# Attention with a feed-forward behind it on one core: the first quad laid out anew, row-norm seeds, transposes and sums moved in the instruction order

**Chip, cores, metric.** One Trainium2 chip (trn2), one of its cores. The metric is the time of one execution in microseconds (us), as the median of several executions; lower is better. Names in profile lines: PE is TensorE (matrix products), PEld its weight loads, DVE is VectorE, ACT is ScalarE, POOL is GpSimd, SPq the queue of SyncE that issues loads. In names of tiles, qk is a pair's loaded q and k, qkn the same normalised, qkT transposed, s its scores, E their exponentials, o its outputs; rc holds the reciprocals of the sums, xT the divided outputs, u and uT the hidden values of the feed-forward and their transposition. The gain of a pair is the scaling of its q by the gains. A clock window is here a stretch of 3.4 us, or a few of them in a row, for which TensorE was granted half its clock. Lanes are slots that loads in flight take up; no trace names them. Every line number is that of the kernel whose profile the line is from; the changed kernel's numbers are about 5 above those of the kernel before.

## The reference, cut to what matters

```python
# q, k, v: (8 batches, 12 heads, 448, 64) fp32;  x: 3584 tokens x 768;  d_ff = 1024
q_n, k_n = rmsnorm(q, g_q), rmsnorm(k, g_k)          # x / sqrt(mean(x*x) + 1e-6) * g
attn = softmax(q_n @ k_n.T / sqrt(64))               # per head
x = (attn @ v) in (batch * seq, heads * 64)
h = x @ w_in
solu = h * softmax(h)
ln = (solu - mean) / sqrt(var + 1e-6) * g_ln
out = ln @ w_out                                     # fp32
```

## The kernel before

It works on head pairs n (48 of them) and on quads m of two pairs, a = 2m and b = 2m + 1. TensorE goes through a quad's scores, values and sums. The other three engines meanwhile prepare the next quad's pairs: squares (ACT), row sums (DVE), a swap of halves and a fold (POOL), the seed of an inverse root (ACT), its step and the normalising (POOL), a transposition (DVE) and the scaling by the gains (ACT), behind which the first scores of a pair wait. They also divide the last quad's outputs and convert pieces of the weights (`begin`, `step`, `end`). From quad 6 on the feed-forward of finished tokens is mixed in, as units of TensorE work with ACT and DVE work behind them.

These are the operations that the change moves:

```python
    def first(n):
        return nc.gpsimd if n else nc.vector

    def swap_sums(n):                                  # row sums of the other half: 4 POOL copies
        d = st[n]
        d["ss"] = small.tile([P, 2 * NB], FP32, tag="ss", name="ss")
        for g in range(4):
            o = g ^ 1
            first(n).tensor_copy(d["ss"][g * 32 : g * 32 + 32], d["part"][o * 32 : o * 32 + 32])

    def fold_sums(n):
        d = st[n]
        first(n).tensor_tensor(d["ss"], d["ss"], d["part"], OP.add)

    def rsqrt_seed(n):                                 # 3 small ACT instructions
        # ... cut
        nc.scalar.activation(d["y"], d["ss"], AF.Ln, scale=1.0 / D, bias=eps)
        nc.scalar.activation(d["x"], d["ss"], AF.Copy, scale=-0.5 / D, bias=-0.5e-6)
        nc.scalar.activation(d["y"], d["y"], AF.Exp, scale=-0.5)

    def inverse(m):                                    # DVE, then 4 POOL copies
        # ... cut
        nc.vector.transpose(r.rearrange("p b i -> p (b i)"), d["sm"])
        nc.vector.reciprocal(rc, r[:, :, 0].rearrange("p b -> p () b").to_broadcast([P, 2, NB]))
        for h in range(2):
            for i in range(2):
                a = 64 * h + 32 * i
                o = 64 * h + 32 * (1 - i)
                nc.gpsimd.tensor_copy(rc[o : o + 32, i], rc[a : a + 32, i])
```

The order of the quad loop, which is the order in which each engine's queue gets its instructions (`W_IN` = 12 and `W_OUT` = 22 are the pairs at which w_in and w_out are converted, so `a < W_OUT` means quads 0 to 10):

```python
            unit(lambda: scores(b, 2))                 # ends with the last exponential of b
            # ... adds cut
            if next1:
                if m:
                    rsqrt_seed(a + 2)
                    rsqrt_step(a + 2)
                    normalise(a + 2)
                rsqrt_seed(b + 2)
                rsqrt_step(b + 2)
            # ... cut: outputs, squares and sums of a + 4, qk_transpose(a + 2), normalise(b + 2),
            #          values(b), squares(b + 4), row_sums(b + 4), gain(a + 2)
            if next2:
                swap_sums(b + 4)
                fold_sums(b + 4)
            unit(lambda: sums(m))
            if a < W_IN and next1:
                qk_transpose(b + 2)
            inverse(m)
            if a >= W_IN and next1:
                qk_transpose(b + 2)
            later(1, lambda m=m: divide(m))            # after the next unit of TensorE work
```

The start, cut: `load_next()` loads one 512 KB piece of w_in.

```python
    load(0); setup(); load(1); load_next(); load_next()
    load(2); load(3); load_v(0); load_next()
    # ... 8 warming products on TensorE, then pairs 0 and 1 prepared, then the loop
```

## Time and profile before

| | before |
|---|---|
| median (the 3 runs that the prediction had) | 1006.16 us (1004.56 to 1006.8) |
| span of the profiled execution | 1004.8 us |
| mean granted clock of TensorE | 0.988 |
| first score product | 18.59 us |
| starts of quads 1, 6, 11 and 12 | 41.67, 123.14, 264.55 and 313.0 us |

A quad's start is its first score product in the timeline of PE. The distance of two starts is a quad's length, and the difference of two kernels' starts is how far one leads by then. The lines of the page, of the waits and of the timeline before stand in the prediction.

### The profile page before, as it was taken

How to read it: one execution, taken by the hardware profiler on the slowest of the kernel's cores; microseconds unless marked ns; L12 is line 12 of the kernel's file. 1: busy time of each engine (PE TensorE's matmuls, PEld its weight loads, DVE VectorE, ACT ScalarE, POOL GpSimd, SP SyncE). 2: the span in 40 equal slices, each digit the busy share in tenths (PEclk: the TensorE clock that was granted, in tenths of full speed). 3: DMA queues.
4: the chain of work that ended last, by engine and by line, in shares of the span. 5: the costliest groups of instructions: out<-in, count | busy, mean ns of one | idle time of the engine just before them, and what ended most of it. 6: DMA issues, size and time to landing. Idle time of an engine off the chain costs nothing.

```text
span 1004.8 us, 11376 instructions
## 1 busy us (share of the span) xinstructions
PE 958.6 (95%) x3907; PEld 431.9 (43%) x3907; DVE 515.3 (51%) x756; ACT 359.4 (36%) x622; POOL 294.0 (29%) x641
## 2 busy tenths in 40 slices
PE   6899898899899999999999999999999999999997
PEld 2232233333344444444444444454444444455554
DVE  3588866667545435454544453526254544466610
ACT  4778655546432323232322332323133233011110
POOL 3475742233423223232414131415141312100000
PEclk9899999999999999999999999999999999999999
DMA  7667653344303021212113030303030100455201
GB/s 153 135 161 137 143 123 82 74 94 87 55 23 65 24 47 34 54 33 54 36 35 71 16 71 16 70 3 71 16 71 16 34 17 19 166 157 159 84 34 49
DMA packets 235956, 70.14 MB, mean 70 GB/s; under 512 B 224968, under 2 KB 225232, under 8 KB 235888
## 3 DMA queue, kind: packets, MB, share of 16 engines
q1 hardware_dynamic: 227840, 57.77, 26.4%
q10 hardware_dynamic: 7888, 11.47, 3.0%
q8 instruction: 33, 0.54, 0.2%
q14 instruction: 35, 0.29, 0.1%
q0 software_dynamic: 160, 0.07, 0.1%
HBM read 58.27 MB, written 11.01 MB: 69 GB/s over the span
## 4 chain that ended last, share of the span: by engine, by line
PE 76%; DVE 8%; POOL 6%; ACT 4%; DMA 3%; issue 2%; SPq 1%; POOLq 0%; DVEq 0%; ACTq 0%
PE po L836 28%; PE h L778 26%; PE s L657 8%; PE o L711 7%; PE pu L825 2%; POOL qkn L626 2%; PE s L670 2%; POOL ss L600 2%; ACT E L647 1%; DVE r L758 1%; PE o L700 1%; DVE xT L760 1%; PE warm L957 1%; PE sm L735 1%; DMA qk<-in_k_dram 1%
## 5 line engine op out<-in xcount | busy, mean ns | idle before, releaser
L778 PE MATMUL h<-w_in,xT 128*128 128x512 f32 x672 | 303.8, 602 | 0.1
L836 PE MATMUL po<-w_out,uT 128*128 128x384 f32 x896 | 298.0, 489 | 1.4 <-ACT uT L826 0.7
L836 PEld LDWEIGHTS po<-w_out,uT 128*128 128x128 f32 x896 | 168.0, 190 | 131.5 <-issue 19.3
L647 ACT ACTIVATE E<-s 128x896 f32<-128x896 f32 x168 | 149.0, 914 | 163.9 <-PE s L657 158.9
L778 PEld LDWEIGHTS h<-w_in,xT 128*128 128x128 f32 x672 | 125.5, 192 | 161.1 <-issue 155.4
L657 PE MATMUL s<-qkT 64*128 64x448 f32 (+1 forms) x768 | 136.9, 574 | 18.8 <-ACT E L647 7.8
L837 ACT COPY y<-po 128x384 f32<-128x384 f32 x56 | 26.8, 478 | 266.9 <-PE po L836 266.9
L711 PE MATMUL o<-E,v 128*64 128x448 f32 x576 | 115.1, 549 | 1.7 <-ACT E L647 1.7
L809 POOL TENSOR_TENSOR he<-he,mhalf 128x1 f32<-128x1 f32 x28 | 18.7, 669 | 291.9 <-DVE he L808 291.7
L687 POOL TENSOR_TENSOR es<-E 128x896 f32<-128x896 f32 x26 | 54.0, 2076 | 147.3 <-ACT E L647 147.3
L690 DVE TENSOR_TENSOR es<-es,E 128x896 f32<-128x896 f32 (+1 forms) x52 | 56.6, 1089 | 64.0 <-ACT E L647 58.5
L657 PEld LDWEIGHTS s<-qkT 64*128 64x128 f32 (+1 forms) x768 | 42.6, 160 | 101.4 <-issue 45.0
L827 DVE COPY uT<-pu 128x512 f32<-128x512 f32 x28 | 19.2, 687 | 130.3 <-PE pu L825 79.2
L626 POOL TENSOR_TENSOR qkn<-qk,ny 128x896 f32<-128x896 f32 x47 | 80.6, 1714 | 10.8 <-DMA v<-in_v_dram 4.8
L788 DVE TENSOR_REDUCE hmax<-h 128x1 f32<-128x1024 f32 x28 | 34.2, 1221 | 77.0 <-PE h L778 77.0
L711 PEld LDWEIGHTS o<-E,v 128*64 128x64 f32 x576 | 39.5, 138 | 76.3 <-issue 67.8
L587 DVE TENSOR_REDUCE part<-sq 128x28 f32<-128x896 f32 x48 | 51.2, 1066 | 40.6 <-ACT sq L582 40.4
L618 POOL TENSOR_TENSOR nx<-nx,ny 128x28 f32<-128x28 f32 x47 | 19.8, 421 | 153.0 <-ACT ny L613 153.0
L636 DVE STREAM_TRANSPOSE qkT<-qkn 128x896 f32<-128x896 f32 x48 | 53.0, 1103 | 21.9 <-POOL qkn L626 21.2
L799 DVE TENSOR_TENSOR u<-h,u 128x1024 f32<-128x1024 f32 x28 | 34.2, 1221 | 50.7 <-ACT u L794 50.7
L582 ACT ACTIVATE sq<-qk 128x896 f32<-128x896 f32 x48 | 45.5, 949 | 36.6 <-DVE part L587 22.8
L758 DVE STREAM_TRANSPOSE r<-rc 128x448 f32<-128x448 f32 x48 | 30.9, 644 | 40.7 <-POOL rc L749 38.2
(90 smaller groups left out, 741.3 us busy)
## 6 DMA issues: line engine op xcount, KB each, us to landing
qk<-in_q_dram SPq DMA_DIRECT2D x192, 56.0 KB, 2.3
out_dram<-y ACTq DMA_DIRECT2D x27, 384.0 KB, 2.3
qk<-in_k_dram SPq DMA_DIRECT2D x184, 56.0 KB, 2.4
v<-in_v_dram SPq DMA_DIRECT2D x96, 96.0 KB, 2.6
raw<-in_moe_w_in_dram SPq DMA_DIRECT2D x12, 512.0 KB, 4.3
raw<-in_moe_w_out_dram SPq DMA_DIRECT2D x16, 384.0 KB, 3.1
again<-in_moe_w_in_dram SPq DMA_DIRECT2D x13, 448.0 KB, 3.9
again<-in_moe_w_out_dram SPq DMA_DIRECT2D x13, 448.0 KB, 4.1
```

Of the source, the lines that this page charges most:

```text
L582: nc.scalar.activation(d["sq"], d["qk"].rearrange("p s b d -> p (s b) d"), AF.Square)
L587: nc.vector.tensor_reduce(d["part"], d["sq"], AX, OP.add)
L626: first(n).tensor_tensor(d["qkn"], d["qk"].rearrange("p s b d -> p (s b) d"), d["y"].rearrange("p b -> p b ()").to_broadcast([P, 2 * NB, 32]),
L636: nc.vector.transpose(d["qkT"].rearrange("p s t -> p (s t)"), d["qkn"].rearrange("p b d -> p (b d)"))
L647: nc.scalar.activation(d["E", kc], s[:, :, 0:S], AF.Exp)
L657: nc.tensor.matmul(s[c : c + w, h, 0:S], d["qkT"][hh, 1, kc * P + c : kc * P + c + w], d["qkT"][hh, 0, :], start=True, stop=True,)
L687: engine.tensor_tensor(d["es"], d["E", 0], d["E", 1], OP.add)
L690: engine.tensor_tensor(d["es"][pp], d["es"][pp], x[pp], OP.add)
L711: nc.tensor.matmul(d["o"][h * D : (h + 1) * D, :], d["v"][:, h, kc], d["E", kc][:, h], start=False, stop=(kc == NJ - 1),)
L758: nc.vector.transpose(r, quads[m]["rc"][:, i].rearrange("p b -> p b ()").to_broadcast([P, NB, 32]))
L778: nc.tensor.matmul(d["h"][:, hs], xTs[m][:, c, i * P : (i + 1) * P], w_in[:, c, hs], start=(c == 0), stop=(c == KD - 1))
L836: nc.tensor.matmul(po, d["uT"][:, c], w_out[:, c, hs], start=(c == 0), stop=(c == KF - 1))
```

## The change

Its intent, in four parts. The first quad gets another order: gains loaded through ACT's queue, squares of pair 0 on DVE, no warming products, one piece of w_in fewer ahead of pairs 2 and 3 and one more behind the first values, pair 3 prepared in smaller steps. The seeds of both next pairs are issued ahead of the last exponential of b (from quad 1 on). The transposition of b's next pair goes ahead of the inverse in quads 6 to 10 too, as it did in quads 0 to 5. And swapping and folding of b's sums go behind the copies of the reciprocals.

The diff, whole:

```diff
@@ -438,13 +438,14 @@
         nc.gpsimd.memset(ones[0:D, 2], 0.0)
         make_identity(nc, ident)
 
+    def load_gains():
         for i, g in enumerate((g_q, g_k)):
-            nc.gpsimd.dma_start(gg[:, i], g.rearrange("(o d) -> o d", o=1).to_broadcast([P, D]))
-            nc.gpsimd.dma_start(
+            nc.scalar.dma_start(gg[:, i], g.rearrange("(o d) -> o d", o=1).to_broadcast([P, D]))
+            nc.scalar.dma_start(
                 grow[KF + i : KF + i + 1].rearrange("o (h d) -> o h d", h=2),
                 g.rearrange("(o d) -> o () d", o=1).to_broadcast([1, 2, D]),
             )
-        nc.gpsimd.dma_start(grow[0:KF, :], moe_g_ln.rearrange("(c p) -> c p", p=P))
+        nc.scalar.dma_start(grow[0:KF, :], moe_g_ln.rearrange("(c p) -> c p", p=P))
 
     def gain_columns():
         pg = ps_t.tile([P, KF + 2], FP32, tag="t", name="pg")
@@ -579,7 +580,11 @@
     def squares(n):
         d = st[n]
         d["sq"] = work.tile([P, 2 * NB, 32], FP32, tag="sq", name="sq", bufs=1)
-        nc.scalar.activation(d["sq"], d["qk"].rearrange("p s b d -> p (s b) d"), AF.Square)
+        qk = d["qk"].rearrange("p s b d -> p (s b) d")
+        if n:
+            nc.scalar.activation(d["sq"], qk, AF.Square)
+        else:
+            nc.vector.tensor_tensor(d["sq"], qk, qk, OP.mult)
 
     def row_sums(n):
         d = st[n]
@@ -935,28 +940,17 @@
 
     N = B * NP
 
-    def prepare(n):
-        squares(n)
-        row_sums(n)
-        swap_sums(n)
-        fold_sums(n)
-
     load(0)
     setup()
     load(1)
-    load_next()
+    load_gains()
     load_next()
     load(2)
     load(3)
     load_v(0)
     load_next()
+    load_next()
     with tc.manual_schedule():
-
-        warm = ps_h.tile([P, DFF], FP32, tag="h", name="warm")
-        for _ in range(8):
-            nc.tensor.matmul(
-                warm[:, 0:S], ident, st[0]["qk"][:, 1].rearrange("p b d -> p (b d)"), start=True, stop=True
-            )
         squares(0)
         row_sums(0)
         swap_sums(0)
@@ -964,21 +958,19 @@
         squares(1)
         row_sums(1)
         rsqrt_seed(0)
-        gain_columns()
-        begin(0)
         rsqrt_step(0)
-        nc.vector.tensor_reduce(gmax, gg[:, 0], AX, OP.max, apply_absolute_value=True)
-        normalise(0)
         swap_sums(1)
         fold_sums(1)
+        gain_columns()
+        normalise(0)
+        nc.vector.tensor_reduce(gmax, gg[:, 0], AX, OP.max, apply_absolute_value=True)
         gain_limit()
         rsqrt_seed(1)
         rsqrt_step(1)
         normalise(1)
         qk_transpose(0)
         gain(0)
-        step(0)
-        end(0)
+        begin(0)
         at = 0
         for m in range(NQ):
             a, b = 2 * m, 2 * m + 1
@@ -1005,6 +997,8 @@
                 step(a)
             else:
                 qk_transpose(1)
+                step(0)
+                end(0)
             unit(lambda: scores(a, 1))
             gain(b)
             if next2:
@@ -1018,10 +1012,10 @@
             if m:
                 end(a)
             else:
-                prepare(2)
-                rsqrt_seed(2)
-                rsqrt_step(2)
-                normalise(2)
+                squares(2)
+                row_sums(2)
+                swap_sums(2)
+                fold_sums(2)
             add(a, 2, DVE)
             ff(1)
             unit(lambda: scores(b, 0))
@@ -1031,23 +1025,26 @@
                 if a >= W_IN:
                     begin(b)
             else:
-                prepare(3)
+                squares(3)
+                row_sums(3)
             add(b, 1, POOL)
             add(a, 3, DVE)
             ff(2)
+            if m and next1:
+                rsqrt_seed(a + 2)
+                rsqrt_seed(b + 2)
             unit(lambda: scores(b, 2))
             add(b, 1, DVE)
             add(b, 3, DVE)
             add(b, 2, DVE)
+            if m == 0:
+                rsqrt_seed(2)
+                begin(1)
             if next1:
+                rsqrt_step(a + 2)
+                normalise(a + 2)
                 if m:
-                    rsqrt_seed(a + 2)
-                    rsqrt_step(a + 2)
-                    normalise(a + 2)
-                rsqrt_seed(b + 2)
-                rsqrt_step(b + 2)
-            if m == 0:
-                begin(1)
+                    rsqrt_step(b + 2)
             step(b)
             unit(outputs)
             if next2:
@@ -1056,6 +1053,11 @@
             end(b)
             if next1:
                 qk_transpose(a + 2)
+                if m == 0:
+                    swap_sums(3)
+                    fold_sums(3)
+                    rsqrt_seed(3)
+                    rsqrt_step(3)
                 if a < W_IN:
                     begin(a + 2)
                 normalise(b + 2)
@@ -1074,15 +1076,15 @@
                     begin(a + 2)
                 if b + 2 < W_IN:
                     begin(b + 2)
+            unit(lambda: sums(m))
+            if a < W_OUT and next1:
+                qk_transpose(b + 2)
+            inverse(m)
+            if a >= W_OUT and next1:
+                qk_transpose(b + 2)
             if next2:
                 swap_sums(b + 4)
                 fold_sums(b + 4)
-            unit(lambda: sums(m))
-            if a < W_IN and next1:
-                qk_transpose(b + 2)
-            inverse(m)
-            if a >= W_IN and next1:
-                qk_transpose(b + 2)
             later(1, lambda m=m: divide(m))
             if next1:
                 load_v(m + 1)
```

## The prediction

> **What bounds the kernel now.** I read the page's busy shares first, then who TensorE waited for in three stretches, then the timeline around the longest of those waits.
>
> ```profile
> span 1004.8 us, 11376 instructions
> PE 958.6 (95%) x3907; PEld 431.9 (43%) x3907; DVE 515.3 (51%) x756; ACT 359.4 (36%) x622; POOL 294.0 (29%) x641
> PE   6899898899899999999999999999999999999997
> ```
>
> TensorE (PE) bounds the kernel: it is busy for 958.6 of 1004.8 us, and from slice 12 on it has almost no idle time. What a reordering can win is the remaining 46 us, plus the 8.7 us of warming products that count as busy and do no work, plus whatever runs at half clock. Nearly all of it lies before 300 us, as the waits of PE show (us in total, times, longest) for 0 to 100 us, 100 to 300 and 300 to the end:
>
> ```profile
> PE s L657 <- ACT qkT L640: 5.5, 4, 2.6
> PE s L657 <- ACT E L647: 5.1, 5, 3.7
> ...
> PE s L670 <- ACT qkT L640: 9.4, 4, 2.9
> PE pu L825 <- DVE xT L760: 2.4, 2, 1.6
> ...
> PE s L657 <- DVE uT L827: 3.2, 3, 1.4
> ```
>
> The parts of the change answer to these waits one by one. A quad m is two head pairs, a = 2m and b = 2m+1. By its first score products, quad 0 runs from 18.59 to 41.67 us, quads 1 to 5 take 16.3 us each, quads 6 to 10 about 30 each with the feed-forward between, and from quad 11 (264 us) PE is full.
>
> **What the Trainium skill says.** "TensorE: Matmul & The Clock Gate", Part 1: the array is at half clock until a free-running window of about 3.4 us was busy, and goes back after an idle one. The trace agrees: the granted clock averages 0.84 in 20 to 30 us and 0.70 in 30 to 40, although eight products warmed the array up to 15.8 us; the first scores at 18.59 take 0.75 us a product, twice the later 0.37. It went cold in the 2.6 us gap behind the warming. The same page, "Architectural detail", calls the queues of ScalarE, VectorE and GpSimd strict FIFO; every argument below rests on that, and the trace shows it (the gain of b stands behind an exponential of the feed-forward, below). "SBUF — State Buffer", "Who interferes with whom": a VectorE instruction with two SBUF inputs, or in a 2-port mode, and a GpSimd instruction that reads SBUF exclude each other. The trace agrees: GpSimd's small multiply takes 0.24 us alone and 0.57 to 1.27 beside VectorE's sums of E.
>
> **Part 1, the first quad.** Here the chain is GpSimd and ScalarE order:
>
> ```profile
> 15.77 0.22 PE L451 MATMUL pg<-ident,grow 10*128 10x10 f32 x1
> 16.03 0.17 ACT L452 COPY gcol<-pg 128x10 f32<-128x10 f32 x1 [4.76 <-PE pg L451]
> 17.89 0.65 ACT L640 ACTIVATE qkT<-qkT,gcol 128x448 f32<-128x448 f32 x1
> 18.59 4.33 PE L657 MATMUL s<-qkT 64*128 64x448 f32 x16 [2.60 <-ACT qkT L640]
> ```
>
> The transposition of the gains waits for the warming products; behind its copy stand the weight conversion (1.4 us) and the seeds of b (0.55). The new order takes all three away from ahead of the gain, but puts five gain loads in ScalarE's queue ahead of the squares of pair 1. The last of these reuses the lane of k's last slice (issued 7.0, about 2.6 to land), so I put the squares at 10.2 instead of 9.73, row sums to 12.3, step 13.1, normalising 14.2, GpSimd's sums of pair 1 and the gain product 14.7, maximum 14.9, VectorE's transposition (1.1) 16.05, gain (0.65) 16.75: first scores at 16.8, 1.8 us earlier. Then the seeds of pair 2 no longer stand between the exponentials (PE waited 3.7 us there). With cold products of 1.5 us a score tile the last exponential of b ends near 28.6 instead of 32.8. But pair 3's sums still come on GpSimd behind the normalising of pair 2 (near 32.3) and ScalarE waits for them: seeds of 3 near 34.0, one conversion 1.4, squares of pair 5 0.95, gain 0.7, quad 1 at about 37.5. Loads give nearly the same bound: pair 5 landed about 35.4 before (last issue 33.1, 2.3 to land), same bytes ahead of it now, then squares and gain make 37.1. I take 38.0 for 41.67: **-3.7 us**. The missing warm-up costs nothing, since the scores were cold already.
>
> **Part 2, quads 1 to 5.** Between two quads:
>
> ```profile
> 45.42 0.89 POOL L749 COPY rc<-rc 32x14 f32<-32x14 f32 x4
> 46.09 0.65 DVE L758 STREAM_TRANSPOSE r<-rc 128x448 f32<-128x448 f32 x1 [1.31 <-POOL rc L749]
> ...
> 49.95 0.31 ACT L611 ACTIVATE ny<-ss,eps 128x28 f32<-128x28 f32 x1
> ...
> 57.13 0.67 ACT L640 ACTIVATE qkT<-qkT,gcol 128x448 f32<-128x448 f32 x1 [1.50 <-DVE qkT L636]
> ...
> 57.85 1.77 PE L657 MATMUL s<-qkT 64*128 64x448 f32 x8 [0.96 <-ACT qkT L640]
> ```
>
> The seeds move ahead of the last exponential (0.92 us), so they start at 49.1, not 49.95. That alone gives little: GpSimd's first step then meets VectorE's sum of E (49.79 to 50.87), and it ended at 50.97 already. The quieter edit matters more: swapping and folding b's sums now come behind the copies of the reciprocals, which were waiting for them. The reciprocal was done at 44.78, so the copies start at 44.85 instead of 45.42, and the whole VectorE chain of dividing, converting and summing moves 0.57 us up, the GpSimd step with it. PE's wait of 0.96 falls to about 0.4. Five starts (quads 2 to 6) at 0.57: **-2.85 us**.
>
> **Part 3, quads 6 to 10.** The wait of 9.4 us:
>
> ```profile
> 149.23 0.89 POOL L749 COPY rc<-rc 32x14 f32<-32x14 f32 x4
> 149.91 0.65 DVE L758 STREAM_TRANSPOSE r<-rc 128x448 f32<-128x448 f32 x1 [2.21 <-POOL rc L749]
> 152.54 1.21 DVE L788 TENSOR_REDUCE hmax<-h 128x1 f32<-128x1024 f32 x1
> 153.79 1.11 ACT L794 ACTIVATE u<-h,hmax 128x1024 f32<-128x1024 f32 x1 [2.10 <-DVE hmax L788]
> 154.90 0.66 ACT L640 ACTIVATE qkT<-qkT,gcol 128x448 f32<-128x448 f32 x1
> 155.60 1.76 PE L670 MATMUL s<-qkT 64*64 64x448 f32 x4 [2.90 <-ACT qkT L640]
> ```
>
> The gain is not late for want of the transposition, done at 147.7, but queued behind the feed-forward's exponential, and that behind maximum, dividing and reciprocal copies. Counted from T, the end of b's normalising (146.56), copies started at T+2.67 behind two sets of sums. Now: transposition 1.1, inverse 1.0 behind it, copies at T+2.2. So the new transposition order alone would cost a microsecond, and the copies ahead of the sums win it back and 0.49 more. T moves up too: seeds 0.8 earlier, of which about 0.45 arrives, because b's normalising waits for VectorE to transpose a (ended 144.73). Together 0.94 for each of four waits: -3.8. The wait of transposes on dividing at quad 11 has the same cause: -0.95. These idle times also sent the clock to one half for 3.4 us in quads 7, 8 and 9 (the mean is 0.94 in each; the last products take 1.76 us instead of 0.97, and the next group 6.16 and 7.10 instead of 5.42), about 1.5 us each; I count on two of the three: -3.0. One wait grows: in quad 10 values already wait 1.7 us for the last exponential, which comes 0.9 later, but dividing ends that stretch, so it is hidden. Sum **-7.75 us**.
>
> **Part 4, from quad 11.** The copies come 1.24 us earlier (0.92 and 0.24 with their gaps), the seeds about a microsecond. This should remove most of the waits on VectorE's copy of uT (3.2 us): **-2.2 us**. All else is PE at work.
>
> **Sum.** 3.7 + 2.85 + 7.75 + 2.2 = 16.5; 1006.16 - 16.5 = 989.7, say **990 us**, a gain of 1.6%.
>
> **Rivals.** (1) The first quad gains little. The gain loads in ScalarE's queue wait for lanes, squares of pair 1 slip, and loads or seeds of pair 3 hold quad 1. For it: ScalarE waited 2.7 us for GpSimd there, and DMA is 0.78 to 0.80 busy to 30 us. Then part 1 gives 0 to 1 and the time is 993. (2) The transposition ahead of the inverse stretches the dividing chain more than the copies save, because VectorE stands waiting for GpSimd's normalising. For it: the gap is only half a microsecond. Then part 3 gives 1 or 2 and the time is about 996. (3) All PE waits go, with their cold windows: 5.5 at the start, 4.75, 9.4 + 4.5 + 2.4, 3.2 make 30 us, 976 us. Against it: only some of each chain is shortened. (4) The last exponential, a microsecond later, stalls values in every quad. Against it: outside quad 10 it is needed only after 4 us of other products.
>
> **Range and chances.** The four terms err mostly alone, the clock windows by chance: 80% within **983.5 to 997.5**. Faster by over 2% means below 986.0, some 4 us under my figure: **0.22**. Within 2%: **0.77**. Slower: **0.01**; nothing is added to TensorE, VectorE gains one 1.1 us square and loses nothing.
>
> **What would show it.** First scores near 16.8 us and quad 1 near 38; quads 1 to 5 at 15.7 us each; copies of reciprocals directly behind the reciprocal; the 9.4 us wait near 5.6; clock below 1.0 in at most one or two windows between 150 and 250; PE busy about 950 us, 8.7 less by the warming. I am wrong if quad 1 starts after 40, if the 9.4 stays or vanishes, or if values wait for the last exponential in many quads.

## The result, and the profile after

The changed kernel takes **990.49 us** (median of 4, 990.15 to 991.6) beside 1006.21 (1004.56 to 1006.8, 4 runs) for the one before: ratio 0.9848, 95% interval 0.9831 to 0.9865. That is 1.5% faster, inside two per cent. The profiled execution spans 988.7 us, 16.1 less than before.

The head of the page of the changed kernel (busy us, share of the span, instructions; then PE's busy tenths in 40 slices):

```profile
span 988.7 us, 11291 instructions
PE 944.8 (96%) x3891; PEld 426.6 (43%) x3891; DVE 510.8 (52%) x757; ACT 355.3 (36%) x621; POOL 297.3 (30%) x636
PE   3699999998999999999999999999999999999997
```

PE is busy 13.8 us less. Warming was 8.7 of that. About half of the rest is products that no longer run at half clock: the warming left out, PE was busy for 19.4 us in half-clock stretches before and for 14.4 now, and full clock halves such time (an estimate from the traces' clock records). The other half is not accounted for. The middle slices went from 8 and 9 in turn to 9.

What PE waited for, in the same three stretches as in the prediction (us in total, times, longest):

```profile
PE s L662 <- ACT qkT L645: 11.5, 3, 7.1
...
PE s L675 <- ACT qkT L645: 4.8, 4, 1.7
...
PE o L716 <- ACT E L652: 2.5, 1, 2.5
...
PE s L662 <- DVE uT L832: 1.3, 3, 0.4
```

The 9.4 us wait on the gain is now 4.8 (L670 before, L675 after), the one on uT 1.3 instead of 3.2, and that on xT is gone from the top. But a wait of 7.1 us on the gain, which the kernel before did not have, is in the first 100 us. The timeline of the changed kernel shows it, in the first quad:

```profile
15.82 3.36 PE L662 MATMUL s<-qkT 64*128 64x448 f32 x8 [4.06 <-ACT qkT L645]
...
21.55 1.54 SPq L477 DMA_DIRECT2D raw<-in_moe_w_in_dram  x3
...
26.48 6.52 SPq L562 DMA_DIRECT2D qk<-in_k_dram  x4
...
34.78 0.95 ACT L585 ACTIVATE sq<-qk 128x896 f32<-128x896 f32 x1 [5.65 <-DMA qk<-in_q_dram]
...
40.84 1.87 PE L662 MATMUL s<-qkT 64*128 64x448 f32 x4 [7.12 <-ACT qkT L645]
```

The first scores come at 15.82 us, 2.8 earlier than before. Then three pieces of w_in are issued in a row, and the loading queue needs 6.52 us to get the four k slices of pair 4 out behind them (3.57 before). The squares of pair 4 stand in ACT's queue until 34.78, the seeds of pair 3 and the rest behind them, and quad 1 starts at 40.84: 0.83 earlier than before, not 2.8. Even that is within the scatter of single executions: with the old first quad, quad 1 starts at 41.32 to 42.32 us in three traces (the kernel before, e4, e12), and with the new one at 40.84 to 41.99 in four (the changed kernel, e1, e2, e3).

Where the time was won, from the starts of the quads:

| stretch | predicted | measured |
|---|---|---|
| to the start of quad 1 | -3.7 | -0.83 |
| quads 1 to 5 | -2.85 | -2.43 |
| quads 6 to 11 | -7.75 | -9.80 |
| from quad 12 | -2.2 | -3.0 |
| whole span | -16.5 | -16.1 |

In quads 6 to 11 the quads as such are 2.7, 2.6 and 2.9 us shorter in 7, 8 and 9, quad 10 is 1.1 us *longer* (25.67 against 24.57), and quad 11 is 2.7 shorter. Quad 6 of the changed kernel into quad 7, in the timeline:

```profile
144.79 0.89 POOL L754 COPY rc<-rc 32x14 f32<-32x14 f32 x4 [0.86 <-DVE rc L749]
145.47 0.65 DVE L763 STREAM_TRANSPOSE r<-rc 128x448 f32<-128x448 f32 x1 [0.81 <-POOL rc L754]
...
150.45 0.66 ACT L645 ACTIVATE qkT<-qkT,gcol 128x448 f32<-128x448 f32 x1
...
151.16 0.97 PE L675 MATMUL s<-qkT 64*64 64x448 f32 x4 [1.71 <-ACT qkT L645]
```

Against the same lines in the prediction: the copies start right behind the reciprocal (their wait is on DVE, no longer on POOL's own queue), PE waits 1.71 us instead of 2.90, and the four products take 0.97 us instead of 1.76, because the clock has not gone to one half.

### The profile page after: what moved, and what is told of

Its sections match the earlier page's. It is cut to its first block, busy times and chain, and to the rows that moved or that the text cites. A ratio compares the mean times of both kernels' runs of the same rounds, so it can differ in the third digit from the quotient of the medians.

```text
span 988.7 us, 11291 instructions
## 1 busy us (share of the span) xinstructions
PE 944.8 (96%) x3891; PEld 426.6 (43%) x3891; DVE 510.8 (52%) x757; ACT 355.3 (36%) x621; POOL 297.3 (30%) x636
## 4 chain that ended last, share of the span: by engine, by line
PE 85%; DVE 4%; DMA 3%; ACT 3%; SPq 2%; POOL 1%; issue 1%; ACTq 0%; DVEq 0%; POOLq 0%
PE po L841 30%; PE h L783 29%; PE o L716 9%; PE s L662 9%; PE pu L830 3%; PE sm L740 2%; PE s L675 2%; ACT E L652 2%; DMA raw<-in_moe_w_in_dram 2%; PE o L705 2%; SPq L562 1%; POOL qkn L631 1%; DVE qkT L641 1%; DMA vl<-in_v_dram 1%; DVE r L763 1%
## 5 line engine op out<-in xcount | busy, mean ns | idle before, releaser
L783 PE MATMUL h<-w_in,xT 128*128 128x512 f32 x672 | 300.6, 597 | 0.1
L662 PE MATMUL s<-qkT 64*128 64x448 f32 (+1 forms) x768 | 139.0, 582 | 19.1 <-ACT qkT L645 12.7
L631 POOL TENSOR_TENSOR qkn<-qk,ny 128x896 f32<-128x896 f32 x47 | 84.6, 1801 | 22.9 <-DMA v<-in_v_dram 14.3
L623 POOL TENSOR_TENSOR nx<-nx,ny 128x28 f32<-128x28 f32 x47 | 17.8, 378 | 106.9 <-ACT ny L618 106.9
L799 ACT ACTIVATE u<-h,hmax 128x1024 f32<-128x1024 f32 x28 | 31.1, 1112 | 49.3 <-DVE hmax L793 49.3
```

What stands on the lines that cost most here:

```text
L631: first(n).tensor_tensor(d["qkn"], d["qk"].rearrange("p s b d -> p (s b) d"), d["y"].rearrange("p b -> p b ()").to_broadcast([P, 2 * NB, 32]),
L662: nc.tensor.matmul(s[c : c + w, h, 0:S], d["qkT"][hh, 1, kc * P + c : kc * P + c + w], d["qkT"][hh, 0, :], start=True, stop=True,)
L783: nc.tensor.matmul(d["h"][:, hs], xTs[m][:, c, i * P : (i + 1) * P], w_in[:, c, hs], start=(c == 0), stop=(c == KD - 1))
```

## The experiments

All kernels gave the right result, and each was timed over five rounds beside the kernel before. There were four sittings; the kernel before had a median of 1006.19, 1005.55, 1006.76 and 1006.37 us in them, so medians of different sittings may be compared to within about a microsecond. The first four runs undo one part each; e5 to e8 test what held the first quad; e9 to e11 put together what won; e12 does one part alone.

### e1: sums back ahead of the reciprocal copies

```diff
+            if next2:
+                swap_sums(b + 4)
+                fold_sums(b + 4)
             unit(lambda: sums(m))
 ...                                  # and taken away behind inverse(m)
```

> The changed kernel (990.5 us) with one thing undone: swapping and folding b's sums stand ahead of the copies of the reciprocals again. Theory (this order is the main gain of quads 2 to 6, the early seeds alone give little): quads 2 to 5 last about 16.2 us again instead of 15.5 to 15.8, the reciprocal copies start 0.5 us later after b's normalising in quads 6 to 10, the waits for VectorE's copy of uT come back: 5 to 7 us slower, about 996.5. Rival (the early seeds carry the gain): under 2 us slower, 991 to 992.5.

**Measured: 998.42 us** (996.69 to 999.86; ratio 0.9926, 0.991 to 0.9941), 7.9 more than the changed kernel. Quads 3 and 5 are 17.02 us each, longer even than the 16.3 of the kernel before. There the early seeds, without the moved sums, let POOL's normalising meet DVE's weight conversion. The timeline of e1 in quad 3 (quad 5 has the same 2.07 us, at 118.81):

```profile
85.60 2.07 DVE L497 SCALAR_TENSOR_TENSOR tmp<-raw,tmp 128x512 uint32<-128x512 uint32 x1
...
88.70 0.95 ACT L585 ACTIVATE sq<-qk 128x896 f32<-128x896 f32 x1 [3.08 <-DVE part L592]
```

The same DVE instruction takes 0.69 us when it does not run beside POOL's normalising (at 81.74, same run). This agrees with the Trainium skill, "SBUF — State Buffer", "Who interferes with whom": a VectorE instruction with two SBUF inputs and a GpSimd instruction that reads SBUF exclude each other, and a normalising of 1.79 us started 0.27 ahead of it. So the order of the sums is worth 8 us in the changed kernel, more than the 5 to 7 that I had put down for it.

### e2: transposes behind the inverse from quad 6 on, as before

```diff
-            if a < W_OUT and next1:
+            if a < W_IN and next1:
                 qk_transpose(b + 2)
             inverse(m)
-            if a >= W_OUT and next1:
+            if a >= W_IN and next1:
```

> The changed kernel with one thing undone: from quad 6 on VectorE transposes b behind the inverse again. Theory (this order by itself lengthens the dividing chain, because VectorE stands waiting for GpSimd before it may invert): the reciprocal copies start at T+1.24 instead of T+2.17 (T: end of b's normalising), the wait of the last scores for the gain falls from 4.8 us to about 1.6, and the kernel is faster than the changed one: about 987.5. Rival (the early transposition is what shortened that wait): the wait grows to 6 us or more, 992 or slower.

**Measured: 986.79 us** (986.42 to 988.43; 0.9815, 0.9799 to 0.9831): **3.7 us faster than the change**. The transposes ahead of the inverse cost time. The timeline of e2, to be held against that of the changed kernel above:

```profile
144.48 0.89 POOL L754 COPY rc<-rc 32x14 f32<-32x14 f32 x4
...
150.85 0.97 PE L675 MATMUL s<-qkT 64*64 64x448 f32 x4 [0.91 <-ACT qkT L645]
```

DVE's transposition of 1.1 us no longer stands ahead of the reciprocal; PE waits 0.91 us for the gain instead of 1.71. Quads 7 and 8 are 0.8 us shorter each, quad 10 is 1.7 shorter, since its wait of 2.2 us for an exponential did not send the clock to one half as the 2.48 us of the changed kernel did. That last part is partly chance: e6, e7 and e8 have the wait of 2.5 us too and keep full clock (see the last section). e9 beside e6, below, gives the cost of the transposes without it.

### e3: seeds behind the last exponential, as before

```diff
-            if m and next1:
-                rsqrt_seed(a + 2)
-                rsqrt_seed(b + 2)
             unit(lambda: scores(b, 2))
 ...
+            if m and next1:
+                rsqrt_seed(a + 2)
+                rsqrt_seed(b + 2)
             if next1:
                 rsqrt_step(a + 2)
```

> The changed kernel with one thing undone: from quad 1 on the seeds stand behind the last exponential again. Theory (the seeds give a part of a microsecond for each quad, and cost 0.8 in quad 10, where values then wait 1.7 instead of 2.5 us for the last exponential and the clock stays full): 1 to 3 us slower, about 992. Rival a (the seeds do most of the work in quads 2 to 10): 5 us or more slower. Rival b (they give nothing): 990.5 or a little under.

**Measured: 996.65 us** (995.35 to 999.23; 0.9916, 0.9899 to 0.9932), 6.2 more than the changed kernel (the profiled executions differ by 4.9). This was more than I had expected; it is the size that rival a gave. Quads 3 to 5 hardly care (15.80 to 15.81 us against 15.49 to 15.82), quad 2 is 0.5 longer; quads 7 to 9 are 0.6 to 0.7 longer each; quad 10 is 1.7 *shorter*, and quad 11 2.5 longer. The two lines of e3's timeline that show both sides of it:

```profile
246.75 0.97 PE L716 MATMUL o<-E,v 128*64 128x448 f32 x4 [1.63 <-ACT E L652]
...
260.07 0.66 PE L830 MATMUL pu<-ident,u 128*128 128x128 f32 x4 [1.11 <-DVE xT L765]
```

and that of the changed kernel in quad 10:

```profile
244.06 1.76 PE L716 MATMUL o<-E,v 128*64 128x448 f32 x4 [2.48 <-ACT E L652]
```

With early seeds the last exponential of quad 10 comes late, values wait 2.48 us and then run at half clock (1.76 us for four products instead of 0.97). Without them the dividing comes late, and the feed-forward's transposes wait for xT. Taken together the early seeds win.

### e4: the old first quad with the three other parts

Made from the kernel before, with the seeds, the transposes and the sums in the new order, but its start and its first quad untouched (warming products included).

> The kernel before with everything but the first quad changed (seeds, transposition order, sums order). Theory (the new first quad gives nearly nothing, since quad 1 started at 40.84 us instead of 41.67 and then ran its first scores at half clock): quad 1 at 41.7, full clock there, whole time within 0.8 us of the changed kernel, 990 to 991.3. Rival (my prediction: the first quad is worth 3.7 us): about 994.

**Measured: 990.64 us** (989.72 to 992.26; 0.9847, 0.9829 to 0.9866), against 990.49. The new first quad is worth nothing in the end. Compared with e4, the changed kernel's first scores come 3.5 us earlier (15.82 against 19.36), but quad 1 starts 1.5 earlier, and quad 2 only 0.3 (57.7 against 58.0). The first scores of e4 come 0.8 us later than those of the kernel before, with the same start, so single starts tell no more than that.

### e5 and e6: fewer pieces of weight ahead of pair 4

```diff
# e5: the start of the kernel before     # e6: two pieces early, the third behind pair 5
     load_gains()
     load_next()
+    load_next()                           (not in e6)
     load(2)
     load(3)
     load_v(0)
     load_next()
-    load_next()
 ...
                 load(b + 4)
+                if m == 0: load_next()    (e6 only)
```

> The changed kernel with the old order of loads alone (two pieces of w_in ahead of pairs 2 and 3, one behind v). Theory (three pieces of w_in in a row ahead of pair 4 hold its slices back on the lanes, its squares hold ScalarE, and so quad 1): ScalarE's wait of 5.65 us for pair 4 mostly goes, quad 1 starts at 37 to 38.5 instead of 40.84, 987 to 988.5. Rival (GpSimd's order, sums of pair 3 behind the normalising of pair 2, is the bound): quad 1 stays within 0.7 us of 40.8, 990 to 991.

> The changed kernel with the third piece of w_in loaded behind pairs 4 and 5. Theory as in the run with the old loads: only two pieces lie ahead of pair 4, quad 1 starts near 37.2, 987. If the lane wait is the cause, this does as well as the old order of loads or better. Rival: quad 1 near 40.8, 990 to 991, or the later piece of w_in makes quad 1 wait in its conversion and gives the gain back.

**Measured: e5 987.62 us** (986.86 to 989.11; 0.9829, 0.9813 to 0.9844), **e6 987.52 us** (986.65 to 988.9; 0.9826, 0.9811 to 0.9841). Both are 3 us faster than the changed kernel. Quad 1 starts at 37.63 and 37.91, where the prediction had it (38.0). The one piece too many in front of pair 4 was the cause. The timeline of e6:

```profile
34.26 0.32 ACT L616 ACTIVATE ny<-ss,eps 128x28 f32<-128x28 f32 x1 [2.38 <-POOL ss L609]
...
36.35 0.95 ACT L585 ACTIVATE sq<-qk 128x896 f32<-128x896 f32 x1 [0.21 <-DMA qk<-in_k_dram]
...
37.91 4.33 PE L662 MATMUL s<-qkT 64*128 64x448 f32 x16 [3.82 <-ACT qkT L645]
```

Now it is the chain that the prediction told: seeds of pair 3 wait for POOL until 34.26, squares of pair 5 at 36.35 (nearly held by their load), gain, quad 1. That a queue in order makes a later transfer wait also fits the Trainium skill, "DMA: Bandwidth & Descriptors", "Queues, rings and completion order", which says that each DMA engine consumes the descriptors of a ring in ring order. Here three pieces of 512 KB stand ahead of slices of 56 KB in one queue. At the 300 GB/s or so that moved at that time (309 from 26 to 28 us in the changed kernel), 1.5 MB are some 5 us (an estimate). How the large pieces hold up the issue of the small ones is not shown; that moving one of them frees pair 4 is.

### e7 and e8: the clock in the first quad

```diff
# e7: eight warming products ahead of squares(0)
# e8: eight products whose result nobody reads, behind the sums of quad 0
             unit(lambda: sums(m))
+            if m == 0:
+                idle = ps_t.tile([P, 2, 512], FP32, tag="t", name="idle")
+                for _ in range(8):
+                    nc.tensor.matmul(idle[:, 0, 0:S], ident, st[b]["E", 0][:, 0], start=True, stop=True)
```

> The changed kernel with the eight warming products put back at its start. Theory (the start of quad 1 is set by the landing of pair 4 and 5, not by the first scores): first scores move by up to 1 us, quad 1 stays at 40.8 within 0.3, time 990.5 within 0.5. Rival (the missing warm-up costs): 1 us or more faster. Rival (the products delay the gains and that counts): 1 us or more slower.

> The changed kernel with eight idle products on TensorE behind the sums of quad 0, into a free score tile that nobody reads. Theory (the 7.1 us of idleness ahead of quad 1 halve the clock for its first 5 us, and that is why quad 1 lasts 16.85 us): quad 1 starts at 40.8 as before, at full clock, and lasts about 15.3; 988.5 to 989.3. Rival (quad 1 is long for another reason): 990 to 991.

**Measured: e7 989.92 us** (989.07 to 991.15; 0.985, 0.9833 to 0.9866), **e8 989.87 us** (987.88 to 990.34; 0.9841, 0.9825 to 0.9858). Neither can be told from the changed kernel by its interval. The warming products were worth nothing, as predicted, although they worked: in e7 PE has full clock from 10.88 to 34.77 us, in the changed kernel only from 21.90. Quad 1 starts at 40.21 in e7, outside the 0.3 us that I had allowed around 40.8. In e8 the clock did stay up: from 40 to 50 us (busy us of PE, PEld, DVE, ACT and POOL with their instructions, then the granted clock, DMA share, GB/s), the changed kernel has

```profile
40.00:50.00 10.00, 8.77 (x44) 3.08 (x48) 8.36 (x13) 8.19 (x14) 3.13 (x15) 0.71 0.75 146
```

and e8 has

```profile
40.00:50.00 10.00, 8.83 (x54) 2.72 (x54) 8.16 (x13) 9.50 (x18) 4.33 (x16) 1.00 0.78 155
```

Quad 1 shrinks from 16.85 to 15.14 us, but starts 0.5 later (its first scores do by 1.2, ahead of anything that e8 changes, so this is scatter), and quad 2 grows from 15.06 to 15.69. That is the length of most quads from 1 to 5: as I read it, once PE is warm the loop of the other engines sets it, and it takes the rest back. Then a half clock costs its full price only where PE alone sets the pace.

### e9, e10, e11: what won, put together

```diff
# e9  = the edit of e2 and that of e6
# e10 = e9 with five idle products behind the sums of quad 0, as in e8
# e11 = e9, and in quad 0 the gain of pair 2 goes ahead of the squares of pair 5
#       and of the conversion of the next piece of weight
+            if m == 0:
+                gain(a + 2)
             if next2:
                 squares(b + 4)
                 row_sums(b + 4)
-            if next1:
+            if m and next1:
                 gain(a + 2)
             step(b)
 ...                                  # begin(2) moves behind step(b) when m == 0
```

> The changed kernel with two edits that each won alone: transposes of b behind the inverse from quad 6 on, as before the change (986.8 us against 990.5, -3.7), and the third early piece of the feed-forward's first weight moved behind the loads of pair 5 (987.5, -3.0). Theory: they act on different waits (the gain's wait behind the reciprocal copies in quads 6 to 9; the loads of pair 4 in the first quad), so they add: 983.8 us, quad 1 at 37.9, quads 6 to 9 as short as 27.1, 27.2, 26.9. That would be a ratio of 0.978 to the kernel before. Rival: whatever comes earlier at quad 1 is taken back by the feed-forward stages' own loops, and the two together give no more than the larger alone, 986.5.

> The same with five idle products behind the sums of the first quad, so that TensorE does not fall to half clock in front of quad 1. TensorE stands 3.8 us there, just over the window, and its first 3.4 us at half clock lengthen quad 1 (16.3 against 15.1 kept warm). Theory: quad 1 falls to about 15.3, but quad 2 takes back 0.5, as it did with the eight idle products alone: 983.2 us, 0.6 below the one without. Rival: it is all taken back: 983.8.

> The two edits, and in the first quad ScalarE scales pair 2 by its gains before it squares pair 5 and before it converts the next piece of weight. In the profile with the third piece late, the gain of pair 2 stands at 37.2 us behind the conversion (1.4) and the squares of pair 5 (0.95, which wait for their load until 36.35), while its transposition is done at 34.6. Theory: gain at 34.8, quad 1 at 35.5 instead of 37.9, TensorE stands only 1.4 us and stays warm; but VectorE and GpSimd come after it with pairs 3 and 5, so quad 2 takes some of it back: of 2.4 us and the 0.9 of clock I expect half, 982.2 us. Rival: the loop through normalising of pair 3 (GpSimd until 38.4) and its gain holds the second half of quad 1, so quad 2 starts when it would have: 983.8 us.

**Measured: e9 985.37 us** (984.16 to 986.59; 0.9796, 0.9783 to 0.9809), **e10 984.06 us** (983.28 to 985.01; 0.9776, 0.9763 to 0.979), **e11 984.71 us** (983.67 to 987.58; 0.9796, 0.9779 to 0.9813). All beat both kernels; e10 is about 2.2% faster than the kernel before, and the only one whose interval lies wholly beyond 2%. The two edits add up in the main: of the 6.7 us they won singly, 5.1 are left by the medians (quad 12 starts 6.2 us earlier in e9's trace than in the changed kernel's). The waits in e9 are 3.2 us on the gain in quads 6 to 9, as in e2. e9 is e6 with the old order of transposes, neither has a clock window between quads 6 and 11, and there e9 takes 176.68 us and e6 179.64: the transposes cost 3.0 us with the chance of the clock taken out. That e10 and e11 improve on e9 is not settled: the intervals overlap, and e10's profiled execution is 0.8 us longer than e9's, because there PE goes to half clock within quad 1 instead of at its start. But that is the slowest of e10's five executions, beside the fastest of e9's; in three of e10's five the mean granted clock is 1.0, so mostly the idle products did keep PE warm. In e11 quad 1 starts at 35.66 instead of 38.15, but

```profile
35.66 3.09 PE L662 MATMUL s<-qkT 64*128 64x448 f32 x8 [2.45 <-ACT qkT L645]
...
40.65 0.98 PE L662 MATMUL s<-qkT 64*64 64x448 f32 x8 [1.90 <-ACT E L652]
```

the products run cold, and then PE waits 1.90 us for an exponential that stands behind two pieces of conversion in ACT's queue. Of 2.5 us, 1.0 are left at quad 2 and 0.6 at quad 12.

### e12: the order of the sums alone

```diff
 # the kernel before, and nothing else:
-            if next2:
-                swap_sums(b + 4)
-                fold_sums(b + 4)
             unit(lambda: sums(m))
 ...
+            if next2:
+                swap_sums(b + 4)
+                fold_sums(b + 4)
             later(1, lambda m=m: divide(m))
```

> The kernel before with one block moved and nothing else: swapping and folding the sums of b behind the copies of the reciprocals. From the runs that undo one part: without the early seeds (sums and transposes only) 996.65, so 9.5 us were left; without the new transposes 3.7 more are won. If the three parts add, sums alone gives 9.5 + 3.7 = 13.2: 993 us, with quads 2 to 6 at about 15.7 us each, quads 7 to 9 near 27.8 instead of 30.6. Rival: the moved-up dividing needs the early seeds to be of use (b's normalising ends the stretch instead), so the block alone gives half, 999 us or more, with quads 7 to 9 above 29.

**Measured: 991.25 us** (990.71 to 991.75; 0.9851, 0.9834 to 0.9867). Three moved lines give 15.1 of the 15.7 us. Quads 2 to 5 take 15.80 to 15.82 us, quads 7 to 9 take 27.69, 27.87 and 26.88. The timeline of e12:

```profile
144.93 0.89 POOL L749 COPY rc<-rc 32x14 f32<-32x14 f32 x4
...
151.30 0.97 PE L670 MATMUL s<-qkT 64*64 64x448 f32 x4 [1.53 <-ACT qkT L640]
```

b's normalising ends at 143.56 here, so the copies start 1.37 behind it, where the kernel before had 2.67 and the changed kernel (normalising ended 142.62) has 2.17. Nothing else of the change was needed for that.

### The parts in one table

| kernel | sums | seeds | transposes | first quad | us |
|---|---|---|---|---|---|
| before | old | old | old | old | 1006.2 |
| e12 | new | old | old | old | 991.25 |
| e4 | new | new | new | old | 990.64 |
| after | new | new | new | new | 990.49 |
| e2 | new | new | old | new | 986.79 |
| e3 | new | old | new | new | 996.65 |
| e1 | old | new | new | new | 998.42 |

The sums give 15. The transposes cost 3.7 with early seeds (after against e2). Without early seeds they cost more: e3 has quads 7 to 10 about 0.8 us longer each than e12, and quad 11 1.2. The seeds, undone alone, cost 6.2 (e3). With the old transposes they are still worth about 4: e2 and e12 differ by the seeds and by the first quad, which e4 shows to give nothing (4.5 us by the medians; from quad 2 to the end the traces of e12 and e2 differ by 4.2, those of e3 and the changed kernel by 4.7). So the seeds win mostly by themselves, and only the smaller part, 1.7 us by the medians, is what they save of the transposes' cost. The parts don't add: undoing them singly would account for 7.9 + 6.2 - 3.7 + 0.2 = 10.6 of the 15.7 us. Not run were seeds alone, and sums with seeds with the old first quad.

## Why the prediction was right or wrong

The time was right (990 against 990.49) and the class too, with errors in the steps that cancelled; that they cancelled was luck.

**Part 1 (-3.7) was wrong.** By its own sign, "I am wrong if quad 1 starts after 40", it fell: quad 1 started at 40.84. The first part of the chain went better than told (first scores at 15.82 instead of 16.8), and the gain loads in ACT's queue, the rival's worry, did no harm. The step that failed is "Loads give nearly the same bound: pair 5 landed about 35.4 before (...), same bytes ahead of it now". The bytes ahead of pair 5 are the same, but one piece of them moved from in front of pair 2 to directly in front of pair 4, together with two others, and the queue of issues stood behind them. Squares of pair 4 (34.78), which the prediction did not look at, waited 5.65 us for their load, and ACT's order did the rest. e5 and e6 show it: with one piece elsewhere, quad 1 starts at 37.6 and 37.9. Rival 1 had the outcome ("part 1 gives 0 to 1") and part of the reason ("loads ... hold quad 1"). To this came a clock window: the 7.12 us gap sent PE to half clock from 38.96 to 45.79 us, the first 4.95 us of quad 1, so that by quad 2 the lead was 0.16 us.

**"The missing warm-up costs nothing"** was right: e7, with the products back, has 989.92 us.

**Part 2 (-2.85) was right in size and mechanism.** 2.43 us from quad 1 to quad 6, or 3.1 from quad 2, since quad 1 itself carries the half clock. Quads of 15.06 to 15.82 us were told as 15.7, and PE's wait for the gain at the starts of quads 2 to 6, 0.96 before, is now at most 0.62 (told: 0.4). That it is the sums and not the seeds that do it ("the quieter edit matters more") is shown by e3 (no early seeds, 15.53 to 15.81) and e12 (sums alone, 15.8).

**Part 3 (-7.75) was right in mechanism and too small.** The copies came at T+2.17 as told (T+2.2). PE's wait on the gain fell from 9.4 to 4.8, where the prediction had 5.6. The half-clock windows of quads 7, 8 and 9 are all gone, where I counted on two. Quad 11 gave 2.7 instead of 0.95. Against these, one step failed: "in quad 10 values already wait 1.7 us for the last exponential (...) so it is hidden". It was not hidden: the wait became 2.48. In this execution a clock window followed and quad 10 got 1.1 us longer, but that was chance: in e6, e7 and e8, with the same order and a wait as long, none followed, and quad 10 takes 24.2 us, 0.4 less than before. What the prediction called rival 4 came true in this one quad.

**A conclusion that was there to be drawn.** The prediction wrote that the transposes alone "would cost a microsecond" a quad and that the copies ahead of the sums win it back "and 0.49 more". Both figures hold nearly (2.17 against 1.37 behind the normalising is 0.8; 2.67 to 1.37 is 1.3). I booked the net value and did not say that the kernel without that part should be the faster one, which e2 shows (-3.7 us). Rival 2 described it and I put it at half a microsecond.

**The seeds were too small in the sum.** "About 0.45 arrives" per quad would be 1.8 us in four quads, and part 4 had about a microsecond from them. Undoing them costs 6.2 us in the runs, of which the profiles show 4.9: 0.9 by quad 6, 1.9 in quads 7 to 9, 2.5 in quad 11 and 1.1 after it, while quad 10 gives 1.7 back. The timed runs show a microsecond more because the profiled execution of e3 is the second fastest of its six (995.41, median 996.65).

**Part 4 (-2.2)** measured -3.0: two later quads went from 52.2 to 50.7 us each, and the wait on uT from 3.2 to 1.3.

So the 2.9 us that part 1 fell short, and 0.4 in part 2, were nearly made up by 2.05 more in part 3 and 0.8 more in part 4. Two readings of the prediction were loose, without bearing on the sum: quads 6 and 10 take 25.75 and 24.57 us, not "about 30", and of the slow GpSimd steps near 51 us the one of 1.27 is another instruction than the multiply (0.28 alone), while the one of 0.57 runs mostly beside VectorE's weight conversion. The range and the 0.77 for "within 2%" held, but a right total was no proof of a right account of the start.

## What to carry to other kernels

Look for the small copies that stand in a queue ahead of what the whole next stage waits for: here five POOL instructions of 1.2 us, needed only a quad later, stood ahead of the reciprocals, and moving three lines gave 15 us, and all the rest of a long diff 0.7 on balance, since one part of it won what another lost. Count a load by what stands directly ahead of it in its own queue, not by the bytes issued until then. And test the parts of a change singly on the chip even when the whole is faster: one part of this one cost 3.7 us.

## What the Trainium skill lacked or had wrong

- "TensorE: Matmul & The Clock Gate", Part 1, gives one idle window of about 3.4 us as what sends the array to half clock, and the table "Why this matters for your kernels" warns of gaps above about 3 us. How idle a window has to be it does not say, and the gap alone does not decide: 2.48 us ahead of the values of quad 10 in the changed kernel and in e5, and 2.45 in e11, were followed by half clock, but 2.48 in e6, 2.49 in e7 and 2.62 in e1 were not. In the kernel before, 1.84 us ahead of quad 9's second group was enough.
- What the runs show about that: in the clock records of every packed trace the changes of the clock lie on one grid of 3.413 us (changed kernel: 38.96 and 243.76 us are 60 steps apart), as the page's free-running window would have it. Of the 3943 windows of the 14 traces that ran at full clock, all 35 in which PE was busy for less than 39% were followed by half clock, none of those above 46.5% was, and of the seven between, two were. A half-clock window was followed by full clock in all 23 cases with PE busy for 81% or more, and in none of the 11 below 75%. In the changed kernel PE is busy for 1.23 of the 3.41 us from 240.35, and half clock follows; in e6 the gap of 2.48 us lies across a border of the grid, the windows from 236.17 and 239.58 have 2.23 and 2.10 us, and nothing follows. The grid lies elsewhere in each trace, so it is chance whether a gap of 2 to 3 us costs a window.
- "TensorE: Matmul & The Clock Gate" prices a cold clock by the time at half clock alone. In e8 a warm clock made quad 1 1.7 us shorter and the time only 0.6 shorter, not more than the spread; no page that I used says to look first at what else sets the pace there.
- "DMA: Bandwidth & Descriptors", "Queues, rings and completion order", has the order within a ring, but no number for what large transfers do to the issue of small ones behind them: four slices of 56 KB took 6.52 us to issue behind three pieces of 512 KB (changed kernel), 3.45 to 4.09 behind two (e5, e6), 1.99 to 2.04 us where nothing large stood ahead (kernel before, at 29.05 and 31.09).
